# Outer-product attention and a squareplus MLP on one core: the attention of later row blocks is dealt between the MLP's matmuls

## The chip, the core and the metric

The kernel runs on one core of a Trainium2 chip. Its engines are TensorE (PE; its weight loads are shown apart as PEld), VectorE (DVE), ScalarE (ACT), GpSimd (POOL) and SyncE (SP, which here only issues transfers). The metric is the device time of one execution in microseconds (us); the median of several runs counts.

## What is computed

```python
f = 1.0 / (1.0 + np.exp(-f_logit))                     # q, k, v, f_logit: [4, 8, 768, 48]
for t in range(S):
    state = f[:, :, t, :, None] * state + np.einsum('bhd,bhe->bhde', k[:, :, t], v[:, :, t])
    y[:, :, t] = np.einsum('bhd,bhde->bhe', q[:, :, t], state)
x = y.transpose(0, 2, 1, 3).reshape(3072, 384)
h = x @ w_in                                           # w_in [384, 2048], w_out [2048, 384]
out = (0.5 * (h + np.sqrt(h * h + 4.0))) @ w_out
```

The recurrence is worked out in chunks of 128 tokens. Within a chunk the running sum of ln(1 + exp(-f_logit)) over the tokens scales q down and k up, so that a masked product of the two gives the chunk's own part, and a state of 48 by 48 per head carries the rest from chunk to chunk.

## The kernel before

There are two stages, one after the other. **Attention** goes by batch `b` (four, each of 768 tokens, 8 heads, 6 chunks). L87 to L90 load one batch of the four inputs; L108 and L111 take Exp and Ln of the whole batch; then, head by head, L119 forms the running sums `ca` in fp32 on PE, L124 and L126 take their two exponentials, L129 and L130 multiply q and k with them on POOL into `qkg`, and L134 to L142 form the chunk's decay `gam`. After that come 3 x 8 rounds of (chunk pair, head), each with tiles of 48 rows or 48 columns: transposes (L154, L155), their copy by ACT (L156), scores (L158), the mask on DVE (L160), the product with v (L163), the product with the state (L166), the new state (L170 to L177), and the cast of the result into `xT` by ACT (L181). In `xT` each head has 64 rows, 48 of them used, so that the first weight has four K tiles for 384 rows (L96 to L106 lay it out so).

**The MLP** goes by blocks of 512 tokens (L189, six of them). For each of 16 column tiles, four matmuls of 128x512 (L195) are followed by Square and Sqrt on ACT (L200, L201) and one operation on DVE (L202) that makes `g`; then four output tiles of 16 matmuls each (L208), their copy (L212) and the store (L213). Its buffers in PSUM are taken only when those of the attention are given back (L183). The order of the engines' work is the scheduler's, by the dependencies and the buffers of the pools.

Of the kernel before, what the change touches and what calls it, by code (L numbers as in the profile page):

```python
# [12 lines left out]


@with_exitstack
def kernel(
# [41 lines left out]
    w_in16 = konst.tile([128, NP, DFF], FP16)
    w_out16 = konst.tile([128, NN, DM], FP16)

    xT = konst.tile([128, NP, NTOK], FP16)

    actx = ExitStack()
    pp_ca = actx.enter_context(tc.tile_pool(name="pp_ca", bufs=1, space=bass.MemoryType.PSUM))
    pp_nl = actx.enter_context(tc.tile_pool(name="pp_nl", bufs=1, space=bass.MemoryType.PSUM))
    pp_tr = actx.enter_context(tc.tile_pool(name="pp_tr", bufs=2, space=bass.MemoryType.PSUM))
    pp_py = actx.enter_context(tc.tile_pool(name="pp_py", bufs=2, space=bass.MemoryType.PSUM))
# [176 lines left out]
```

## Time and profile before

| | |
|---|---|
| median of 3 runs | 463.24 us (463.15 to 464.77) |
| span of the profiled execution, first to last instruction | 459.8 us |
| attention stage, 0 to 305 us: PE, DVE, ACT busy | 241.4, 131.3, 139.4 us |
| MLP stage, 305 to 459.8 us: PE, DVE, ACT busy | 149.1, 75.7, 100.0 us |
| PE busy over the whole span | 390.5 us (85%), 2304 matmuls |
| moved by transfers | 30.3 MB |

The profiled execution's own device time is not listed apart from its span; the median is 3.4 us longer than that span, and those 3.4 us are taken to lie before the first and behind the last instruction. A busy PE is not a PE at its peak: a matmul is counted from its first operand read to its modelled end, so overlapping short matmuls fill the line while the array does little. The distance from one start to the next says more.

### The profile page before, as it was taken

How to read it: one execution, taken by the hardware profiler on the slowest of the kernel's cores; microseconds unless marked ns; L12 is line 12 of the kernel's file. 1: busy time of each engine (PE TensorE's matmuls, PEld its weight loads, DVE VectorE, ACT ScalarE, POOL GpSimd, SP SyncE). 2: the span in 40 equal slices, each digit the busy share in tenths (PEclk: the TensorE clock that was granted, in tenths of full speed). 3: DMA queues.
4: the chain of work that ended last, by engine and by line, in shares of the span. 5: the costliest groups of instructions: out<-in, count | busy, mean ns of one | idle time of the engine just before them, and what ended most of it. 6: DMA issues, size and time to landing. Idle time of an engine off the chain costs nothing.

```text
span 459.8 us, 6306 instructions
## 1 busy us (share of the span) xinstructions
PE 390.5 (85%) x2304; PEld 217.6 (47%) x2304; DVE 207.0 (45%) x639; ACT 239.4 (52%) x498; POOL 70.7 (15%) x84
## 2 busy tenths in 40 slices
PE   0064034999999999998999999999999999999997
PEld 0033012656565565645656555534545454544543
DVE  4353015543435623466433464426364554546362
ACT  1440022684445944458644464459292947658390
POOL 6042008101224011171022220000000000000000
PEclk9999999999999999997555555569999999999999
DMA  8999995790006950007300000000101000010101
GB/s 247 227 187 175 152 177 103 135 175 2 0 2 125 184 106 0 2 0 142 66 1 1 0 1 1 2 0 0 70 0 53 18 36 34 19 51 2 70 0 70
DMA packets 30896, 30.30 MB, mean 66 GB/s; under 512 B 784, under 2 KB 30480, under 8 KB 30480
## 3 DMA queue, kind: packets, MB, share of 16 engines
q1 hardware_dynamic: 28288, 23.60, 25.9%
q10 hardware_dynamic: 2576, 6.29, 6.7%
q8 instruction: 18, 0.29, 0.3%
q14 instruction: 14, 0.11, 0.1%
HBM read 25.17 MB, written 4.72 MB: 65 GB/s over the span
## 4 chain that ended last, share of the span: by engine, by line
PE 73%; DMA 9%; ACT 5%; SPq 5%; DVE 3%; POOL 2%; issue 2%; DVEq 0%; ACTq 0%
PE ht L195 14%; PE op L208 14%; DMA vb<-in_v_dram 9%; PE py L166 8%; PE ca L119 7%; PE py L163 7%; PE py L158 6%; PE nl L134 5%; PE tr L154 5%; PE tr L155 4%; SPq L88 3%; PE kv L170 3%; ACT hsq L200 2%; ACT r L201 2%; SPq L89 1%
## 5 line engine op out<-in xcount | busy, mean ns | idle before, releaser
L195 PE MATMUL ht<-xT,w_in 128*128 128x512 f16 x384 | 91.9, 386 | 2.2 <-DVE g L202 2.2
L202 DVE SCALAR_TENSOR_TENSOR g<-ht,r 128x512 f16<-128x512 f32 x96 | 62.3, 687 | 46.9 <-ACT r L201 46.9
L160 DVE TENSOR_TENSOR pmt<-py,mask 128x256 f16<-128x256 f32 x96 | 40.3, 423 | 84.1 <-PE py L158 83.3
L200 ACT ACTIVATE hsq<-ht 128x512 f16<-128x512 f32 x96 | 53.9, 629 | 43.3 <-PE ht L195 43.2
L181 ACT CAST xT<-py 48x256 f16<-48x256 f32 x96 | 34.9, 363 | 73.0 <-PE py L166 67.6
L208 PE MATMUL op<-w_out,g 128*128 128x384 f16 x384 | 69.3, 326 | 0.1
L166 PE MATMUL py<-qkT,shat 48*48 48x128 f16 x160 | 47.5, 297 | 21.4 <-DVE shat L177 21.3
L119 PE MATMUL ca<-lsb,wcent 128*128 128x288 f32 x64 | 41.9, 758 | 25.3 <-ACT lsb L111 24.2
L195 PEld LDWEIGHTS <-w_in 128*128 128x128 f16 x384 | 37.5, 98 | 48.8 <-issue 8.1
L155 PE MATMUL tr<-ident,qkg 128*48 128x128 f16 x192 | 50.2, 306 | 11.6 <-POOL qkg L130 11.6
L201 ACT ACTIVATE r<-hsq 128x512 f16<-128x512 f16 x96 | 57.8, 673 | 0.3
L156 ACT COPY qkT<-tr 48x512 f16<-48x512 f16 x96 | 54.1, 577 | 6.5 <-PE kv L170 3.0
L163 PE MATMUL py<-pmt,v16b 128*48 128x128 f16 x192 | 51.8, 300 | 1.1 <-POOL v16b L114 0.6
L208 PEld LDWEIGHTS <-g 128*128 128x128 f16 x384 | 36.9, 98 | 29.2 <-DVE g L202 3.4
L154 PE MATMUL tr<-ident,qkg 128*48 128x128 f16 x192 | 49.2, 297 | 0.2 <-POOL qkg L129 0.2
L129 POOL TENSOR_TENSOR qkg<-qb,ea 128x288 f16<-128x288 f32 x32 | 25.3, 792 | 137.6 <-ACT ea L124 137.6
L177 DVE TENSOR_SCALAR shat<-tmps,gam 48x48 f16<-48x48 f32 x160 | 41.9, 285 | 0.9 <-DVE tmps L174 0.2
L166 PEld LDWEIGHTS <-shat 48*48 48x48 f16 x160 | 17.9, 112 | 44.3 <-DVE shat L177 22.3
L158 PE MATMUL py<-qkT 48*128 48x128 f16 x192 | 37.7, 293 | 0.0
L134 PEld LDWEIGHTS nl<-hvec,lsb 128*48 128x48 f32 x384 | 34.0, 193 | 5.4 <-issue 3.2
L134 PE MATMUL nl<-hvec,lsb 128*48 128x2 f32 x384 | 35.9, 220 | 0.5 <-DVE nlsb L139 0.5
L163 PEld LDWEIGHTS <-v16b 128*48 128x48 f16 x192 | 23.1, 129 | 24.6 <-issue 15.0
(41 smaller groups left out, 317.0 us busy)
## 6 DMA issues: line engine op xcount, KB each, us to landing
out_dram<-o_sb SPq DMA_DIRECT2D x24, 192.0 KB, 1.9
w_out_f<-in_moe_w_out_dram ACTq DMA_DIRECT2D x1, 3072.0 KB, 16.5
w_in_f<-in_moe_w_in_dram ACTq DMA_DIRECT2D x8, 384.0 KB, 13.0
flb<-in_f_logit_dram SPq DMA_DIRECT2D x4, 0.2 KB, 16.4
qb<-in_q_dram SPq DMA_DIRECT2D x4, 0.2 KB, 10.6
kb<-in_k_dram SPq DMA_DIRECT2D x4, 0.2 KB, 14.6
vb<-in_v_dram SPq DMA_DIRECT2D x4, 0.2 KB, 12.2
```

What stands on the lines that cost most here:

```text
L119: nc.tensor.matmul(out=ca.rearrange("p c d -> p (c d)"), lhsT=wcent, rhs=lsb[:, h].rearrange("p c d -> p (c d)"), start=True, stop=True)
L134: nc.tensor.matmul(out=nl[:, c, :], lhsT=lsb[:, h, c, :], rhs=hvec, start=True, stop=True)
L154: nc.tensor.transpose(out=tr[:, 0, cc, :], in_=qkg[:, h, c, 0:D], identity=ident16)
L155: nc.tensor.transpose(out=tr[:, 1, cc, :], in_=qkg[:, h, c, D:2 * D], identity=ident16)
L158: nc.tensor.matmul(out=pt[:, cc, :], lhsT=qkT[:, 1, cc, :], rhs=qkT[:, 0, cc, :], start=True, stop=True)
L163: nc.tensor.matmul(out=y[:, cc, :], lhsT=v16b[:, h, c, :], rhs=pmt[:, cc, :], start=True, stop=(c == 0))
L166: nc.tensor.matmul(out=y[:, cc, :], lhsT=shat[:, h, c, :], rhs=qkT[:, 0, cc, :], start=False, stop=True)
L195: nc.tensor.matmul(out=ht, lhsT=w_in16[:, j, jn * 128:(jn + 1) * 128], rhs=xT[:, j, tok0:tok0 + MB], start=(j == 0), stop=(j == NP - 1))
L200: nc.scalar.activation(out=hsq, in_=ht, func=AF.Square, scale=1.0)
L201: nc.scalar.activation(out=r16, in_=hsq, func=AF.Sqrt, scale=0.25, bias=1.0)
L202: nc.vector.scalar_tensor_tensor(out=g16[:, jn, :], in0=ht, scalar=0.5, in1=r16, op0=ALU.mult, op1=ALU.add)
L208: nc.tensor.matmul(out=op, lhsT=g16[:, jn, tg * 128:(tg + 1) * 128], rhs=w_out16[:, jn, :], start=(jn == 0), stop=(jn == NN - 1))
```

## The change

The kernel is written anew around row blocks of 128 tokens over all 8 heads (24 of them, 12 pairs). Heads are taken in pairs, each with 64 of 128 columns, so that a transpose or a state product covers two heads (`st_T`, `st_SC`, `st_KV`, `st_Y`); the result is transposed back (`st_YT`) to a dense `xT` of three K tiles. The running sums are two fp16 matmuls, of the high and the low part of the logarithm, in place of one fp32 matmul. Exp and Ln come in seven groups of row blocks (`window`), with a table load ahead of each and one behind. The MLP goes by pairs of row blocks (256 tokens): `mlp1` in eight halves of six 128x256 matmuls, the second matmul (`mlp2`) in quarters of four. The driver issues one group's window, and then the `mlp1` of the group before with the attention steps of the new group between its halves; quarters of `mlp2` fill the windows. The four PSUM tiles `hps` serve `mlp1` and the running sums; four more serve everything else. Weights are loaded in quarters behind the first inputs. The order of ACT is the written one; that of the others is the scheduler's.

```diff
+GROUPS = [(0, 2), (2, 4), (4, 6), (6, 10), (10, 16), (16, 22), (22, 24)]
...
+    ctx.enter_context(tc.manual_schedule(engines={mybir.EngineType.Activation}))
...
+    qt = [konst.tile([128, PR, H, 64], FP16, name=f"qt{i}") for i in range(NB)]
+    kt = [konst.tile([128, PR, H, 64], FP16, name=f"kt{i}") for i in range(NB)]
...
+    hps = [pp_h.tile([128, 512], FP32, name=f"hps{i}") for i in range(4)]
...
+    def load_pair(p):
...
+            for r in range(PR):
+                b, c = divmod(p * PR + r, NC)
+                nc.sync.dma_start(out=got[name][:, r],
+                                  in_=src[b][:, c * C:(c + 1) * C, :].rearrange("h t d -> t h d"))
...
+    def load_w_in(i):
...
+        nc.sync.dma_start(out=s3, in_=moe_w_in[:, i * WQ:(i + 1) * WQ].rearrange("(j p) n -> p j n", p=128))
+        nc.scalar.copy(out=w_in16[:, :, i * WQ:(i + 1) * WQ], in_=s3)
...
+        def exp_ln(p):
...
+            nc.scalar.activation(out=f, in_=f, func=AF.Exp, scale=-1.0)
+            nc.scalar.activation(out=ls, in_=f, func=AF.Ln, bias=1.0, scale=1.0)
+            hi, lo = lhi[p % 2], llo[p % 2]
+            nc.vector.tensor_copy(out=hi[:, :, :, 0:D], in_=ls)
+            nc.vector.tensor_tensor(out=lo[:, :, :, 0:D], in0=ls, in1=hi[:, :, :, 0:D], op=ALU.subtract)
...
+            nc.gpsimd.tensor_copy(out=v16, in_=loads[p]["v"])
...
+        def cums(p):
...
+            for r in range(PR):
+                ca = hp2[r][:, 0:H * D]
+                nc.tensor.matmul(out=ca, lhsT=wcent, rhs=hi[:, r, :, 0:D], start=True, stop=False)
+                nc.tensor.matmul(out=ca, lhsT=wcent, rhs=lo[:, r, :, 0:D], start=False, stop=True)
...
+            for r in range(PR):
+                ca = hp2[r][:, 0:H * D]
+                nc.scalar.activation(out=ea[:, r].rearrange("p h d -> p (h d)"), in_=ca, func=AF.Exp, scale=-1.0)
+                nc.scalar.activation(out=eap[:, r].rearrange("p h d -> p (h d)"), in_=ca, func=AF.Exp, scale=1.0)
+            nc.gpsimd.tensor_tensor(out=qt[p % NB][:, :, :, 0:D], in0=ld["q"], in1=ea, op=ALU.mult)
+            nc.gpsimd.tensor_tensor(out=kt[p % NB][:, :, :, 0:D], in0=ld["k"], in1=eap, op=ALU.mult)
...
+                for hp in range(NP):
+                    o = nl[:, hp, :]
+                    nc.tensor.matmul(out=o, lhsT=hi[:, r, 2 * hp:2 * hp + 2, :], rhs=hvec, start=True, stop=False)
+                    nc.tensor.matmul(out=o, lhsT=lo[:, r, 2 * hp:2 * hp + 2, :], rhs=hvec, start=False, stop=True)
+                nc.vector.tensor_copy(out=nls[b % 2][:, c + r], in_=nl)
...
+    def st_T(r):
...
+        tr = pp_a.tile([128, 2 * NP, C], FP16, name="tr", tag="a")
+        for j in range(NP):
+            nc.tensor.transpose(out=tr[:, j, :], in_=qt[p % NB][:, i, 2 * j:2 * j + 2, :], identity=ident16)
+            nc.tensor.transpose(out=tr[:, NP + j, :], in_=kt[p % NB][:, i, 2 * j:2 * j + 2, :], identity=ident16)
+        qkT = bp.tile([128, 2 * NP, C], FP16, name="qkT", tag="qkT")
+        nc.vector.tensor_copy(out=qkT, in_=tr)
...
+    def st_SC(r):
...
+        for s in range(2):
+            sc = pp_a.tile([128, NP, C], FP32, name="sc", tag="a")
+            o = 64 * s
+            for j in range(NP):
+                nc.tensor.matmul(out=sc[:, j, :], lhsT=qkT[o:o + D, NP + j, :], rhs=qkT[o:o + D, j, :],
...
+            nc.vector.tensor_tensor(out=pm[:, s], in0=sc, in1=mask16.unsqueeze(1).broadcast_to([128, NP, C]),
...
+    def st_KV(r):
...
+        u = pp_a.tile([128, NP, 2, D], FP32, name="u", tag="a")
+        if c > 0:
+            nc.tensor.matmul(out=u.rearrange("p a b d -> p (a b d)"), lhsT=ident16,
+                             rhs=state[r].rearrange("p a b d -> p (a b d)"), start=True, stop=False)
+        for j in range(NP):
+            nc.tensor.matmul(out=u[:, j], lhsT=kt[p % NB][:, i, 2 * j:2 * j + 2, :],
+                             rhs=v16s[p][:, i, 2 * j:2 * j + 2, :], start=(c == 0), stop=(c == 0 or j == NP - 1))
+        sn = bp.tile([128, NP, 2, D], FP16, name="sn", tag="sn")
+        nc.vector.tensor_tensor(out=sn, in0=u,
+                                in1=gam[b % 2][:, c].unsqueeze(3).broadcast_to([128, NP, 2, D]), op=ALU.mult)
...
+    def st_Y(r):
...
+        y = pp_a.tile([128, NP, 2, D], FP32, name="y", tag="a")
+        for j in range(NP):
+            if c > 0:
+                nc.tensor.matmul(out=y[:, j], lhsT=qkT[:, j, :], rhs=state[r][:, j], start=True, stop=False)
+            for s in range(2):
+                nc.tensor.matmul(out=y[:, j, s], lhsT=pm[:, s, j, :], rhs=v16s[p][:, i, 2 * j + s, :],
+                                 start=(c == 0), stop=(c == 0 or s == 1))
+        y16 = bp.tile([128, NJ, 128], FP16, name="y16", tag="y16")
+        nc.vector.tensor_copy(out=y16.rearrange("p a b -> p (a b)"), in_=y.rearrange("p a b d -> p (a b d)"))
...
+    def st_YT(r):
...
+        for j in range(NJ):
+            nc.tensor.transpose(out=yt[:, j, :], in_=part[r]["y16"][:, j, :], identity=ident16)
...
+        nc.vector.tensor_copy(out=xTs[p][:, :, i * C:(i + 1) * C], in_=yt)
...
+        for i in range(n):
+            r = r0 + i
+            at.setdefault(4 * i, []).append((None, lambda r=r: st_T(r)))
+            at.setdefault(4 * i + 2, []).append((None, lambda r=r: st_SC(r)))
+            at.setdefault(4 * i + 5, []).append((None, lambda r=r: st_Y(r)))
+            if (r + 1) % NC and r + 1 < r1:
+                at.setdefault(4 * i + 3, []).append((None, lambda r=r: st_KV(r)))
+            if r == r0 and r % NC:
+                at.setdefault(0, []).append((None, lambda r=r: st_KV(r - 1)))
+            at.setdefault(4 * i + 8, []).append((r, lambda r=r: st_YT(r)))
...
+        def half(j2):
...
+            hb = hps[j2 % 4].rearrange("p (a t) -> p a t", a=2)
+            for a in range(2):
+                jn = 2 * j2 + a
+                for j in range(NJ):
+                    nc.tensor.matmul(out=hb[:, a, :], lhsT=w_in16[:, j, jn * 128:(jn + 1) * 128],
+                                     rhs=x[:, j, :], start=(j == 0), stop=(j == NJ - 1))
...
+        def elem(j4):
...
+            for a in range(2):
+                nc.scalar.activation(out=hsq[:, a, :], in_=hps[(2 * j4 + a) % 4], func=AF.Square, scale=1.0)
             nc.scalar.activation(out=r16, in_=hsq, func=AF.Sqrt, scale=0.25, bias=1.0)
...
+            for a in range(2):
+                jn = 4 * j4 + 2 * a
+                nc.vector.scalar_tensor_tensor(out=g16[:, jn:jn + 2, :].rearrange("p a t -> p (a t)"),
+                                               in0=hps[(2 * j4 + a) % 4], scalar=0.5, in1=r16[:, a, :],
+                                               op0=ALU.mult, op1=ALU.add)
...
+            def quarter(n, i=i, box=box):
...
+                for jn in range(4 * n, 4 * n + 4):
+                    nc.tensor.matmul(out=o, lhsT=gts[p][:, jn, i * C:(i + 1) * C], rhs=w_out16[:, jn, :],
+                                     start=(jn == 0), stop=(jn == NN - 1))
...
+                    nc.vector.tensor_copy(out=o_sb, in_=o)
+                    t0 = (p * PR + i) * C
+                    nc.sync.dma_start(out=out[t0:t0 + C, :], in_=o_sb)
...
+    def run_window(g, per=1):
+        nc.scalar.preload_act_table_set("natural_log_exp_and_others")
+        for s in window(g):
+            s()
+            fill_some(per)
+        nc.scalar.preload_act_table_set("sqrt_and_others")
...
+            for n, s in enumerate(mlp1(p)):
+                s()
+                if n % 3 != 2:
+                    k_half += 1
+                    want = natt * k_half // nhalf
+                    if not att:
+                        fill_some(1)
+                    while att and natt - len(att) < want:
+                        att_slot()
+            fill.extend(mlp2(p))
...
+    more_loads(2)
+    run_window(0)
+    run_window(1)
+    for i in range(4):
+        load_w_in(i)
+    more_loads(3)
+    while att:
+        att_slot()
+    run_mlp1(0)
+    for i in range(4):
+        load_w_out(i)
+    more_loads(6)
+    run_mlp1(1)
+    run_window(2, 2)
+    while att:
+        att_slot()
+        fill_some(2)
+    run_window(3, 2)
+    run_mlp1(2)
+    for g in range(3, NG):
+        if g + 1 < NG:
+            run_window(g + 1, 2)
+        run_mlp1(g)
+    while fill:
```

Three places show how it stands now. First PE in the middle of the program. Before, in the attention stage, a round of one head and two chunks:

```order
L163 LDWEIGHTS v16b
L163 MATMUL py<-pmt,v16b 48x128
L166 LDWEIGHTS shat
L166 MATMUL py<-qkT,shat 48x128
L158 LDWEIGHTS qkT
L158 MATMUL py<-qkT 128x128
...
L170 LDWEIGHTS qkg
L170 MATMUL kv<-v16b,qkg 48x48
L154 LDWEIGHTS qkg
L154 MATMUL tr<-ident_58,qkg 48x128
L155 LDWEIGHTS qkg
L155 MATMUL tr<-ident_58,qkg 48x128
```

In the changed kernel, about two thirds through, `hps` being the tiles of the first matmul, `sc` the scores, `u` the new state, `yt` and `tr` transposes:

```order
L299 LDWEIGHTS w_in_104
L299 MATMUL hps_137<-xT,w_in_104 128x256
...
L218 LDWEIGHTS qkT
L218 MATMUL sc<-qkT 128x128
...
L229 LDWEIGHTS ident_87
L229 MATMUL u<-sn,ident_87 128x384
L232 LDWEIGHTS kt_111
L232 MATMUL u<-v_1966,kt_111 128x96
...
L299 MATMUL hps_138<-xT,w_in_104 128x256
...
L299 MATMUL hps_139<-xT,w_in_104 128x256
...
L258 LDWEIGHTS y_2399
L258 MATMUL yt<-ident_87,y_2399 128x128
```

What moved: the first matmul of the MLP, which stood behind all attention, now stands between the steps of later row blocks, six at a time, and the steps are 128 columns wide.

Second DVE at the same place, `g` made for the MLP, the others for attention. Before, in the attention stage:

```order
L141 TENSOR_TENSOR gamin<-tmp_1753,nlsb 48x5
L140 TENSOR_TENSOR tmp_1775<-nlsb 48x6
L139 COPY nlsb<-nl 48x12
L160 TENSOR_TENSOR pmt<-py,mask_69 128x256
L176 TENSOR_TENSOR tmps<-kv,shat 48x48 x2
...
L177 TENSOR_SCALAR shat<-tmps,gam 48x48 x2
```

and in the changed kernel:

```order
L310 SCALAR_TENSOR_TENSOR g_2322<-hps_138,r_2402 128x512
L310 SCALAR_TENSOR_TENSOR g_2322<-hps_139,r_2402 128x512
L220 TENSOR_TENSOR pm<-sc,mask_92 128x512 x2
L235 TENSOR_TENSOR sn<-u,gam_119 128x384
L310 SCALAR_TENSOR_TENSOR g_2322<-hps_136,r_2442 128x512
L310 SCALAR_TENSOR_TENSOR g_2322<-hps_137,r_2442 128x512
L261 COPY xT<-yt 128x3x128
L208 COPY qkT<-tr 128x1024
L251 CAST y_2490<-y 128x384
```

What moved: DVE makes `g` and the attention's tiles in one queue, two of `g` at a time, and each pair stands behind Sqrt on ACT; the copy `qkT`, which was ACT's, is now DVE's.

Third PE early in the program, in the second pair's first matmul (`o` is an output tile, `g_471` the first pair's `g`):

```order
L299 MATMUL hps_137<-xT,w_in_104 128x256
L328 LDWEIGHTS g_471
L328 MATMUL o<-w_out_105,g_471 128x384
...
L299 LDWEIGHTS w_in_104
L299 MATMUL hps_138<-xT,w_in_104 128x256
```

What moved: the first quarter of the second matmul, which needs the first quarter of `w_out`, stands ahead of halves of the first matmul that don't; the other three quarters follow within the next 130 matmuls. Before, the whole of `w_out` had been loaded and cast long ahead of its first use.

## Rows read from the trace of the kernel before

**Rows 1.** Busy time by stretch: length, PE, PEld, DVE, ACT, POOL, clock, DMA, GB/s

```profile
0.00:305.00 305.00, 241.37 (x1543) 143.82 (x1544) 131.29 (x519) 139.36 (x304) 70.72 (x84) 0.85 0.45 83
305.00:459.80 154.80, 149.14 (x762) 73.80 (x762) 75.72 (x120) 100.04 (x194) 0.00 (x0) 0.99 0.09 31
```

**Rows 2.** The page's chain that ended last, share of the span by engine

```profile
PE 73%; DMA 9%; ACT 5%; SPq 5%; DVE 3%; POOL 2%; issue 2%; DVEq 0%; ACTq 0%
```

**Rows 3.** Busy time by stretch again, columns as in rows 1, for TensorE's pace

```profile
80.00:200.00 120.00, 117.05 (x777) 72.10 (x778) 55.09 (x263) 67.23 (x149) 26.64 (x33) 1.00 0.39 70
...
208.00:210.00 2.00, 1.40 (x14) 0.87 (x13) 1.31 (x6) 0.92 (x3) 1.15 (x2) 1.00 0.01 2
212.00:300.00 88.00, 87.29 (x549) 50.99 (x547) 40.63 (x191) 47.30 (x105) 12.48 (x16) 0.50 0.13 23
...
309.00:460.00 151.00, 145.79 (x752) 72.64 (x751) 75.33 (x120) 96.11 (x189) 0.00 (x0) 1.00 0.09 32
```

**Rows 4.** Timeline of PE in the attention stage: start us, duration us, line, tiles

```profile
202.89 0.31 PE L154 MATMUL tr<-ident,qkg 128*48 128x128 f16 x1
202.99 0.31 PE L155 MATMUL tr<-ident,qkg 128*48 128x128 f16 x1
...
205.28 0.22 PE L154 MATMUL tr<-ident,qkg 128*48 128x128 f16 x1
205.34 0.22 PE L155 MATMUL tr<-ident,qkg 128*48 128x128 f16 x1
...
216.68 0.30 PE L166 MATMUL py<-qkT,shat 48*48 48x128 f16 x1
216.91 0.30 PE L163 MATMUL py<-pmt,v16b 128*48 128x128 f16 x1
```

**Rows 5.** Chain of work in order of time, one MLP block: start, length

```profile
336.42 1.89 PE ht L195 x8
...
348.48 7.49 PE op L208 x45
```

**Rows 6.** Timeline of one MLP block's beginning: start us, duration us, engine, line

```profile
306.17 0.15 PEld L195 LDWEIGHTS <-w_in 128*128 128x128 f16 x1 [0.28 <-issue]
306.59 0.15 PEld L195 LDWEIGHTS <-w_in 128*128 128x128 f16 x1 [0.28 <-issue]
...
311.89 1.16 ACT L201 ACTIVATE r<-hsq 128x512 f16<-128x512 f16 x2
312.56 1.29 DVE L202 SCALAR_TENSOR_TENSOR g<-ht,r 128x512 f16<-128x512 f32 x2 [0.72 <-ACT r L201]
...
313.88 1.18 ACT L201 ACTIVATE r<-hsq 128x512 f16<-128x512 f16 x2
```

**Rows 7.** Groups by line: shapes, count, busy us, mean ns, idle before

```profile
L202 DVE SCALAR_TENSOR_TENSOR g<-ht,r 128x512 f16<-128x512 f32 x96 | 62.3, 687 | 46.9 <-ACT r L201 46.9
...
L160 DVE TENSOR_TENSOR pmt<-py,mask 128x256 f16<-128x256 f32 x96 | 40.3, 423 | 84.1 <-PE py L158 83.3
...
L129 POOL TENSOR_TENSOR qkg<-qb,ea 128x288 f16<-128x288 f32 x32 | 25.3, 792 | 137.6 <-ACT ea L124 137.6
...
L212 DVE COPY o_sb<-op 128x384 f32<-128x384 f32 x24 | 13.4, 558 | 31.9 <-PE op L208 31.9
L124 ACT ACTIVATE ea<-ca 128x288 f32<-128x288 f32 x32 | 13.1, 410 | 36.4 <-PE ca L119 36.2
...
L98 DVE CAST w_out<-w_out_f 128x6144 f16<-128x6144 f32 x1 | 3.4, 3361 | 9.8 <-DMA w_out_f<-in_moe_w_out_dram 9.8
```

**Rows 8.** Busy time by stretch, columns as in rows 1, while inputs load

```profile
30.00:40.00 10.00, 7.03 (x62) 5.59 (x62) 3.57 (x10) 1.64 (x4) 5.91 (x6) 1.00 1.12 188
40.00:60.00 20.00, 0.68 (x5) 0.40 (x5) 0.25 (x2) 0.00 (x0) 0.04 (x1) 1.00 1.05 159
```

**Rows 9.** Timeline of ACT between Exp and Ln: start us, duration us

```profile
20.49 1.28 ACT L111 ACT_TABLE_LOAD   x1
21.79 2.12 ACT L111 ACTIVATE lsb<-lsb 128x2304 f32<-128x2304 f32 x1
```

More of the change, by code (lines that the diff above doesn't have):

```diff
@@ L12 @@
 ALU = mybir.AluOpType
+PSUM = bass.MemoryType.PSUM
+GROUPS = [(0, 2), (2, 4), (4, 6), (6, 10), (10, 16), (16, 22), (22, 24)]
 @with_exitstack
@@ L58 @@
[L58 to L67, printed above, removed]
@@ new lines @@
+    llo = [konst.tile([128, PR, H, 64], FP16, name=f"llo{i}") for i in range(2)]
+    gam = [konst.tile([128, NC, NP, 2], FP32, name=f"gam{i}") for i in range(2)]
+    nls = [konst.tile([128, NC, NP, 2], FP32, name=f"nls{i}") for i in range(2)]
+    for t in lhi + llo:
+        nc.vector.memset(t[:, :, :, D:64], 0.0)
+    for t in gam:
+        nc.vector.memset(t, 0.0)
+    for t in qt + kt:
+        nc.gpsimd.memset(t[:, :, :, D:64], 0.0)
+    hps = [pp_h.tile([128, 512], FP32, name=f"hps{i}") for i in range(4)]
@@ new lines @@
+    state = {}
+    xTs = {}
+    part = {}
+    def st_T(r):
+        p, i = divmod(r, PR)
+        tr = pp_a.tile([128, 2 * NP, C], FP16, name="tr", tag="a")
[4 more added lines that the diff above has]
+        nc.vector.tensor_copy(out=qkT, in_=tr)
+        part[r] = {"qkT": qkT}
@@ new lines, in mlp2 @@
+    def mlp2(p):
+        steps = []
+        for i in range(PR):
+            box = {}
+            def quarter(n, i=i, box=box):
+                if n == 0:
+                    box["o"] = pp_a.tile([128, DM], FP32, name="o", tag="a")
+                o = box["o"]
+                for jn in range(4 * n, 4 * n + 4):
+                    nc.tensor.matmul(out=o, lhsT=gts[p][:, jn, i * C:(i + 1) * C], rhs=w_out16[:, jn, :],
+                                     start=(jn == 0), stop=(jn == NN - 1))
+                if n == 3:
+                    o_sb = mp.tile([128, DM], FP32, name="o_sb", tag="o_sb")
+                    nc.vector.tensor_copy(out=o_sb, in_=o)
+                    t0 = (p * PR + i) * C
+                    nc.sync.dma_start(out=out[t0:t0 + C, :], in_=o_sb)
+            steps += [lambda n=n, q=quarter: q(n) for n in range(4)]
+        return steps
@@ new lines, with more_loads, att_slot, fill_some @@
+    NG = len(GROUPS)
+    pairs_of = [list(range(a // PR, b // PR)) for a, b in GROUPS]
+    nload = 0
+    def more_loads(upto):
+        nonlocal nload
+        while nload < min(upto, NRB // PR):
+            load_pair(nload)
+            nload += 1
+    att = []
+    done_x = set()
+    fill = []
+    def att_slot():
+        if att:
+            for r, s in att.pop(0):
+                s()
+                if r is not None:
+                    done_x.add(r)
+    def fill_some(n):
+        for _ in range(n):
+            if fill:
+                fill.pop(0)()
@@ new lines @@
+    more_loads(2)
[13 more added lines that the diff above has]
+    while att:
+        att_slot()
+        fill_some(2)
[6 more added lines that the diff above has]
+    while fill:
+        fill_some(1)
```

276 lines of the change are left out of this document (130 added, 146 removed).

## The prediction

> **What bounds the kernel now.** I read the busy time by stretch first. The program has two halves that don't overlap: attention to about 305 us, the MLP for the 155 us after it [rows 1]. The chain of waits says that PE carries 73% of it [rows 2]. But the reader should not take that for a PE at its limit. In the attention stage PE shows 117 of 120 us busy with 777 matmuls between 80 and 200 us [rows 3], that is 0.15 us each, for tiles of 128 columns or fewer. The timeline shows why: back-to-back transposes start 0.10 us apart at 202.9 us and 0.06 apart at 205.3, and where a product with the state (48 rows) and one with v (128 rows) alternate, the starts lie 0.23 us apart [rows 4]. So small tiles and a slow clock fill this stage. The record of the clock says 1.00 from the start, but the pace at 202.9 us is that of 0.50 further on; only from about 205 to 212 us is it the faster one. I read it so: the attention stage runs at the lower level (1.2 GHz) except for those 7 us, which end after a stretch with PE 1.40 of 2.00 us busy; after that the record says 0.50 to 300 us and the pace is 549 matmuls in 88 us, about the same as before [rows 3]. In the MLP stage, dense from 309 us, it stays at 1.00 (2.4 GHz) to the end [rows 3].
>
> **Prices.** *PE*: eight 128x512 matmuls take 1.89 us and forty-five 128x384 take 7.49 us [rows 5], so 0.166 us for 384 columns and 0.11 for 256 at the upper level; at the lower one 512 columns go 0.42 us apart (the weight loads of 306.17 and 306.59 us [rows 6]), so 0.21 for 256 and 0.32 for 384. An attention step is 0.06 or 0.107 us [rows 4]; the alternation at 0.23 is the upper bound, nothing below 0.055 is seen. A row block has 36 of them (8 in `st_T`, 8 in `st_SC`, 5 in `st_KV`, 12 in `st_Y`, 3 in `st_YT`): 2.2 us at the upper level, 3.9 at the lower, 8.3 at the bound. I take the spacing of transposes, since all but the 8 scores use all rows of the array. *ACT*: Square and Sqrt of two 512-column tiles repeat every 1.99 us [rows 6], which is the price of one `elem`; there are 48, 96 us. Exp of 288 columns is 0.41 us [rows 7], 0.5 for 384, and of 768 about 0.8, a third of 2.12 with its fixed part [rows 9]. *DVE*: two `g` operations take 1.29 us [rows 6]; a 256-column product from PSUM 0.42, a 384-column copy 0.56 [rows 7], so 0.69 for 512 and 1.22 for the 1024 columns of `qkT`. With two masks and three 384-column tiles a row block costs DVE 4.3 us; back to back I take 4.2. The cast of 6144 columns at 0.55 ns each [rows 7] puts a lower bound of 0.6 us on `qkT`; I take the upper, as its source is in PSUM like L212's. *POOL*: 288 columns are 0.79 us [rows 7], 768 then 2.1, two per pair. *Transfers*: 188 and 159 GB/s with nothing but such 192-byte runs in flight [rows 8]; I take 180, so 8.7 us for a pair's 1.57 MB.
>
> What is removed: two fp32 passes of the running sums, 96 rounds of one head, ACT's copies (L156, L181), and a quarter of the first matmul (three K tiles for four: 576 matmuls of 0.11 us are 63 us, for 384 of 0.22, 83 us). What is added: 24 identity products for the state, 72 transposes back, the split into high and low parts (two DVE passes of 768 columns, 1.4 us a pair). Table loads go from 10 to 14. Each is 1.28 us with ACT's next instruction right behind it, 20.49 to 21.79 us [rows 9], so 18 us in all, some of it while PE does `mlp2`. The Trainium skill, ScalarE: Activation LUTs, What ACT_TABLE_LOAD costs, counts about 2.7 us for a switch, a drain included, and advises to batch by table set; by that the fourteen would be 37 us. Here the trace has no gap around the load, so the row's price stands.
>
> Sums by engine: PE 198 us at the upper level (63 + 64 for the second matmul + 52 for 24 row blocks + 19 for the running sums) and 375 at the lower; DVE 200 (62 + 101 + 13 for the output copies + 24 for windows and casts); ACT 167 (96 + 24 + 19 + 18 + 10). None is near 460, and all three are needed at once, so I sum stretch by stretch in the order of the program.
>
> - **Opening, 92 us.** The third piece of PE's order decides it. Ahead of the last quarter of `w_out` the queue moves pairs 0 to 2, `w_in`, `w_out` and a bit, 11.2 MB: 62 us. The first matmul of pairs 0 and 1 lies under this (their attention is through at 41 us, bound by Exp, POOL and DVE). PE has then some 27 queued 384-column matmuls, 0.32 each at the lower level: 8. The second window's running sums, exponentials and POOL: 6. Two row blocks with nothing beside them: 8 us of latency (2.7 us of T, scores and masks, 2.6 of their DVE work, Y and its transposes 2.7) and 4.2 for the second: 12. The first sums of the next window: 4.
> - **Group (6, 10) with `mlp1` of pair 2, 26 us**: DVE 8 x 0.645 + 4 x 4.2 = 22, PE 26 at the lower level, 14 at the upper. PE is not dense here, so I take the lower.
> - **Group (10, 16), 12 + 42 us.** Of the window 12 us show: table, four Exp/Ln (4.5), `mlp2` matmuls that stand ahead of the sums on PE (2.6), two exponentials pairs (2), POOL (4.2), less overlaps. Then six row blocks with 16 halves: DVE 10.3 + 25.2 = 36, PE 24 or 44. I take 42.
> - **Group (16, 22), 11 + 49 us**: DVE 15.5 + 25.2 = 41, PE 30 or 57; 49 lies between, for an engine that waits in order for two others.
> - **Last group, 7 + 62 us.** One pair's window, and then `mlp1` of four pairs, two row blocks and 13 or 14 output tiles: PE 4 x 5.3 + 4.4 + 36 = 62 at the upper level, as dense as the MLP stage is now; ACT's 32 lie under it.
> - **End, 3 us**: the last copy and store.
>
> That is 304 us of span. Its counterpart is 459.8, and what lies around it, 3.4 us by the median of the runs, comes on top: **307 us**.
>
> **Rivals.**
> *All well overlapped, 259 us.* PE gets to the upper level in the mixed stretches, DVE copies `qkT` and `xT` faster than L212's pace, windows vanish behind `mlp2`: 85 + 20 + 9 + 31 + 8 + 36 + 5 + 58 + 3 = 255. For it: ACT and DVE each total 200 us or less. Against it: DVE and PE wait for each other in order, four `hps` tiles are two `elem` deep, and PE fell back to the lower level at 212 us after short idle times [rows 3]. The Trainium skill, VectorE: DVE Perf Modes, The perf-mode tier table, allows a copy from PSUM up to twice the base rate; by it `qkT` would cost some 0.65 us and a row block 3.5, with 17 us less on DVE in all. No row here has a 16-bit copy from PSUM on DVE.
> *Dealt in name only, 337 us.* The change doesn't do what it says: attention and MLP take turns, because each step waits for DVE while DVE's head waits for Sqrt (`g` at the head of its queue in the second place shown). Then a row block costs its chain of some 6 us and each `mlp1` its 8.2: 92 + 32 + 12 + 52 + 11 + 61 + 7 + 64 + 3 = 334. For it: DVE's 46.9 us of waiting for L201 [rows 7] are that wait in the MLP before, where nothing stands behind it. Against it: the order gives most steps two or more halves of distance.
> *Lower level to the end, 386 us.* The MLP bursts of six never bring the clock up: 95 + 28 + 13 + 46 + 12 + 59 + 9 + 118 + 3 = 383. Against it: the last group is as dense as the stage that holds 1.00 now.
> *Slower than before, about 500 us.* One mechanism: every one of the 1,065 matmuls outside the MLP starts 0.23 us after the last, as where tile heights alternate [rows 4], at the lower clock: 245 + 247 for the MLP + 16 until the first tile = 508. It decides from 0.19 us each on. Against it: runs of equal height are at 0.10 or 0.06.
>
> **How the numbers follow.** Chances: my forecast 0.45 (its own range 288 to 326), all overlapped 0.26, dealt in name only 0.20, lower level 0.06, slower 0.02, other 0.01. The range of 264 to 352 us takes in the first, the third and half or more of the second, with the unknown prices of `qkT` and of the attention's matmuls, and leaves out 2 in 10. Changes under 0.5% can't be told from none here. Every case but one is far below 461 us: faster 0.97, same 0.01, slower 0.02.
>
> **What would show it.** Right: the last `w_out` cast near 62 us and the second window's Exp just behind; DVE and PE both over 80% busy from 130 to 230 us; a clock that changes level in the mixed stretches and stays at 1.00 over the last 60; about 200 us of DVE. `qkT` rows tell the DVE price, the spacing in `st_Y` the PE price. Wrong: DVE waiting for L307 and PE for DVE in turn for tens of us (in name only); a window that leaves all engines idle for 15 us; or a later group's inputs that are not there when its Exp comes, since loads of pairs 6 and 7 stand behind stores in SP's queue.

## The result, and the profile after

The kernel after takes 271.11 us (median of 4 runs, 269.83 to 271.85), the kernel before beside it 463.59: a ratio of 0.585 (95% interval 0.583 to 0.587). The profiled execution took 270.39 us, its span is 268.6. Ratios here and below rest on undisturbed executions alone. The forecast of 307 us was 36 too long: the time lies inside the range, but below the 288 to 326 us that the likeliest case had for itself.

The page of the kernel after (busy time by engine; PE, DVE and the clock in 40 slices of 6.7 us; the chain by engine):

```profile
span 268.6 us, 5160 instructions
PE 213.1 (79%) x2024; PEld 148.9 (55%) x2024; DVE 182.7 (68%) x332; ACT 169.3 (63%) x252; POOL 57.5 (21%) x52
...
PE   0366939897688775986886869999886999999995
...
DVE  1456726863583899579999666999983697645521
...
PEclk9999995999555997999999989999998899999999
...
PE 32%; DVE 22%; ACT 16%; DMA 10%; issue 8%; SPq 6%; POOL 4%; POOLq 1%; ACTq 0%; DVEq 0%
```

PE carries 32% of the chain now, where it carried 73% [rows 2]; DVE and ACT share it. DVE reads 9 from 121 to 148 and from 168 to 195 us (slices 18 to 21 and 25 to 28, counted from 0), PE without a break from 208 us on (slice 31). The clock is down to 0.5 from 40 to 47 and from 67 to 87 us. The row reads 9 for the first 32 us too, but the spacing of the transposes speaks against it:

```profile
17.07 0.31 PE L205 MATMUL tr<-ident,qt 128*128 128x128 f16 x1
17.17 0.31 PE L206 MATMUL tr<-ident,kt 128*128 128x128 f16 x1
...
178.50 0.22 PE L205 MATMUL tr<-ident,qt 128*128 128x128 f16 x1
178.56 0.22 PE L206 MATMUL tr<-ident,kt 128*128 128x128 f16 x1
```

0.10 and 0.06 us apart are the two paces of [rows 4], so PE ran at the lower level (1.2 GHz) at 17 us, as the prediction reads it for the kernel before, whose row reads 9 there too.

The same execution by the stretches of the prediction's sum (columns as in rows 1; a window is taken from DVE's last copy or `g` of the group before to about its first `qkT`):

```profile
0.00:85.50 85.50, 57.40 (x484) 38.04 (x485) 45.73 (x92) 49.43 (x71) 23.20 (x31) 0.85 1.04 197
85.50:105.40 19.90, 13.48 (x167) 9.96 (x166) 18.96 (x34) 14.81 (x20) 3.29 (x3) 0.93 0.60 118
105.40:118.00 12.60, 11.14 (x103) 6.87 (x102) 9.03 (x15) 6.02 (x14) 7.13 (x5) 0.91 1.40 198
118.00:147.50 29.50, 22.87 (x303) 17.86 (x300) 28.29 (x53) 22.66 (x35) 7.75 (x7) 1.00 1.04 165
147.50:165.20 17.70, 14.81 (x128) 8.92 (x127) 11.41 (x18) 8.98 (x21) 11.73 (x6) 0.90 0.10 35
165.20:197.60 32.40, 30.06 (x360) 23.84 (x359) 31.87 (x59) 29.08 (x39) 0.82 (x1) 1.00 0.01 2
197.60:206.00 8.40, 5.06 (x47) 2.90 (x44) 4.30 (x9) 4.67 (x9) 3.56 (x2) 1.00 0.13 47
206.00:265.60 59.60, 58.25 (x447) 40.56 (x447) 32.77 (x56) 33.68 (x49) 0.01 (x1) 0.97 0.11 41
265.60:268.60 3.00, 0.00 (x0) 0.00 (x0) 0.30 (x1) 0.00 (x0) 0.00 (x0) 0.90 0.18 66
```

| stretch | predicted | measured |
|---|---|---|
| opening | 92 | 85.5 |
| (6, 10) with `mlp1` of one pair | 26 | 19.9 |
| window, (10, 16) with two pairs | 12 + 42 | 12.6 + 29.5 |
| window, (16, 22) with three pairs | 11 + 49 | 17.7 + 32.4 |
| window, the rest | 7 + 62 | 8.4 + 59.6 |
| end | 3 | 3.0 |

The three mixed stretches gave 35.2 us less than predicted, the opening 6.5 less, the windows 8.7 more. In the mixed stretches DVE is busy for 79.1 of 81.8 us. What it does there, on its timeline (start, length):

```profile
179.96 0.34 DVE L261 COPY xT<-yt 128x384 f16<-128x384 f16 x1
180.22 0.68 DVE L208 COPY qkT<-tr 128x1024 f16<-128x1024 f16 x1
180.82 0.54 DVE L251 CAST y<-y 128x384 f16<-128x384 f32 x1
181.29 1.27 DVE L310 SCALAR_TENSOR_TENSOR g<-hps,r 128x512 f16<-128x512 f32 x2
182.48 1.27 DVE L220 TENSOR_TENSOR pm<-sc,mask 128x512 f16<-128x512 f32 x2
183.68 0.54 DVE L235 TENSOR_TENSOR sn<-u,gam 128x384 f16<-128x384 f32 x1
184.14 1.27 DVE L310 SCALAR_TENSOR_TENSOR g<-hps,r 128x512 f16<-128x512 f32 x2
185.34 0.34 DVE L261 COPY xT<-yt 128x384 f16<-128x384 f16 x1
```

From one `xT` to the next it is 5.38 us: one row block and four `g`, and each instruction starts as the one before ends or a little sooner (`qkT` 0.26 us after `xT`, which is 0.34 long). By this DVE sets the pace; the doubled copy below tests it.

### The profile page after: what moved, and what is told of

It is laid out like the page before. It is cut to its first block, busy times and chain, and to the rows that moved or that the text cites. A ratio compares the mean times of both kernels' runs of the same rounds, so it can differ in the third digit from the quotient of the medians.

```text
span 268.6 us, 5160 instructions
## 1 busy us (share of the span) xinstructions
PE 213.1 (79%) x2024; PEld 148.9 (55%) x2024; DVE 182.7 (68%) x332; ACT 169.3 (63%) x252; POOL 57.5 (21%) x52
## 4 chain that ended last, share of the span: by engine, by line
PE 32%; DVE 22%; ACT 16%; DMA 10%; issue 8%; SPq 6%; POOL 4%; POOLq 1%; ACTq 0%; DVEq 0%
PE o L328 16%; PE hps L299 10%; SPq L104 6%; DVE g L310 6%; ACT hsq L306 4%; DVE pm L220 3%; ACT r L307 3%; DMA ld_v<-in_v_dram 3%; DMA ld_f<-in_f_logit_dram 3%; DMA w_st<-in_moe_w_in_dram 3%; DVE qkT L208 2%; DVE llo L138 2%; POOL kt L158 2%; DVE y L251 2%; ACT L371 2%
## 5 line engine op out<-in xcount | busy, mean ns | idle before, releaser
L299 PE MATMUL hps<-xT,w_in 128*128 128x256 f16 x576 | 80.5, 285 | 10.6 <-DVE g L310 9.7
L310 DVE SCALAR_TENSOR_TENSOR g<-hps,r 128x512 f16<-128x512 f32 x96 | 61.8, 682 | 20.5 <-ACT r L307 20.5
L328 PE MATMUL o<-w_out,g 128*128 128x384 f16 x384 | 73.0, 335 | 0.2 <-DVE w_out L120 0.2
L299 PEld LDWEIGHTS <-w_in 128*128 128x128 f16 x576 | 57.0, 102 | 23.5 <-issue 13.2
L306 ACT ACTIVATE hsq<-hps 128x512 f16<-128x512 f32 x96 | 54.5, 590 | 23.4 <-PE hps L299 22.3
L307 ACT ACTIVATE r<-hsq 128x1024 f16<-128x1024 f16 x48 | 50.7, 1057 | 1.5
L328 PEld LDWEIGHTS <-g 128*128 128x128 f16 x384 | 37.6, 100 | 23.4 <-issue 3.3
L157 POOL TENSOR_TENSOR qt<-ld_q,ea 128x768 f16<-128x768 f32 x12 | 22.7, 1892 | 82.4 <-ACT ea L155 72.6
L220 DVE TENSOR_TENSOR pm<-sc,mask 128x512 f16<-128x512 f32 x48 | 30.9, 682 | 4.2 <-PE sc L218 4.2
L158 POOL TENSOR_TENSOR kt<-ld_k,eap 128x768 f16<-128x768 f32 x12 | 22.4, 1866 | 0.0
L205 PE MATMUL tr<-ident,qt 128*128 128x128 f16 x96 | 16.7, 245 | 4.6 <-POOL qt L157 3.8
```

The costliest lines, as they stand in the source:

```text
L157: nc.gpsimd.tensor_tensor(out=qt[p % NB][:, :, :, 0:D], in0=ld["q"], in1=ea, op=ALU.mult)
L158: nc.gpsimd.tensor_tensor(out=kt[p % NB][:, :, :, 0:D], in0=ld["k"], in1=eap, op=ALU.mult)
L205: nc.tensor.transpose(out=tr[:, j, :], in_=qt[p % NB][:, i, 2 * j:2 * j + 2, :], identity=ident16)
L220: nc.vector.tensor_tensor(out=pm[:, s], in0=sc, in1=mask16.unsqueeze(1).broadcast_to([128, NP, C]), op=ALU.mult)
L299: nc.tensor.matmul(out=hb[:, a, :], lhsT=w_in16[:, j, jn * 128:(jn + 1) * 128], rhs=x[:, j, :], start=(j == 0), stop=(j == NJ - 1))
L306: nc.scalar.activation(out=hsq[:, a, :], in_=hps[(2 * j4 + a) % 4], func=AF.Square, scale=1.0)
```

## The experiments

Each is the kernel after with the edit shown, timed against the kernel before; "below" and "above after" compare the two ratios. The table splits each profiled span at the loads of the Sqrt table behind the windows of (6, 10), (10, 16), (16, 22) and (22, 24) (us):

| kernel | to 1st | to 2nd | to 3rd | to 4th | to the end | median |
|---|---|---|---|---|---|---|
| after | 87.7 | 34.4 | 42.9 | 39.8 | 63.8 | 271.1 |
| attention in one piece | 86.8 | 38.8 | 52.4 | 50.6 | 51.8 | 282.2 |
| `qkT` copied twice | 87.1 | 38.7 | 47.1 | 43.0 | 65.2 | 283.5 |
| four K tiles | 92.3 | 35.6 | 46.7 | 42.4 | 71.6 | 288.0 |
| `qt`, `kt` on DVE | 85.0 | 34.5 | 40.9 | 39.9 | 61.2 | 263.5 |
| a quarter of the weights | 82.2 | 35.8 | 43.0 | 41.4 | 65.3 | 268.5 |
| single heads | 87.1 | 36.0 | 44.4 | 39.8 | 64.7 | 273.7 |
| early dealing | 79.1 | 36.4 | 43.4 | 39.8 | 64.4 | 265.0 |

**Attention in one piece.**

```diff
         att.extend(attention(g))
+        if g >= 2:
+            while att:
+                att_slot()
-    xp = ... name="xp", bufs=5
+    xp = ... name="xp", bufs=6
```

> The kernel after, with each group's attention issued in one piece behind its window instead of being dealt between the halves of the MLP of the group before (one more buffer for xT). Theory A, the overlap is the gain: 18 row blocks at about 4 us (the spacing of two row blocks alone in the opening of the kernel after, plus latency) are no longer beside 6 pairs of MLP, so the stretches from 85 to 206 us (121 us now) become about 150, and the time about 300 us, 290 to 320. Theory B, the gain comes from the denser tiles and the cheaper steps alone and the dealing adds little: 268 to 276 us.

282.17 us, ratio 0.610 (0.608 to 0.613), 11 us above after: between the theories, and nearer to B. The DVE timeline of its third attention, and then the stretch of this attention and that of the MLP behind it:

```profile
183.41 0.35 DVE L261 COPY xT<-yt 128x384 f16<-128x384 f16 x1
183.67 0.68 DVE L208 COPY qkT<-tr 128x1024 f16<-128x1024 f16 x1
184.27 0.55 DVE L251 CAST y<-y 128x384 f16<-128x384 f32 x1
184.84 1.29 DVE L220 TENSOR_TENSOR pm<-sc,mask 128x512 f16<-128x512 f32 x2
186.04 0.55 DVE L235 TENSOR_TENSOR sn<-u,gam 128x384 f16<-128x384 f32 x1
186.51 0.35 DVE L261 COPY xT<-yt 128x384 f16<-128x384 f16 x1
```

```profile
178.00:195.00 17.00, 11.59 (x174) 8.28 (x172) 16.85 (x34) 6.08 (x9) 0.00 (x0) 0.97 0.01 2
195.00:219.90 24.90, 24.90 (x185) 18.44 (x184) 14.58 (x24) 20.82 (x31) 0.00 (x0) 0.95 0.07 24
```

A row block alone takes 3.10 us here, from one `xT` (183.41) to the next (186.51), and DVE has no gap: DVE sets the pace of the attention by itself too. And the MLP alone is not a chain that waits: PE is 24.9 of 24.9 us busy from 195 us, because `mlp2` of earlier pairs stands between the halves. The table shows the trade: without dealing the second, third and fourth parts grow by 4.4, 9.5 and 10.8 us, and the rest gains 12.0, since part of the second matmuls is done by then.

**`qkT` copied twice.**

```diff
+        qkT2 = bp.tile([128, 2 * NP, C], FP16, name="qkT2", tag="qkT2")
+        nc.vector.tensor_copy(out=qkT2, in_=tr)
         nc.vector.tensor_copy(out=qkT, in_=tr)
```

> The kernel after, with the copy of the eight transposes (qkT, 0.68 us) done twice, the first time into a tile that nobody reads: DVE pays about 1.3 us per row block, a little over what the prediction assumed (1.22). Theory A, DVE sets the pace of the mixed stretches (it is 79 of 82 us busy there): 16 row blocks times 0.6 us, 10 us more, and up to 4 for the six row blocks of the opening: 280 to 285 us. Theory B, the forecast missed by the clock and by waits, not by DVE's prices: 270 to 274 us.

283.53 us, ratio 0.613 (0.609 to 0.618): A. Parts two to four of the table grow by 4.3, 4.2 and 3.2 us, 11.7 for 16 row blocks at 0.6 to 0.7 us. In the second and third part the clock is lower as well; in the fourth, near 1.00 in both kernels, it is 3.2 us for 6 copies. So DVE's time is paid in full there, and the forecast's price for `qkT` (1.22 us for 0.68, 16 times) was worth some 9 to 10 of its 36 us.

**Four K tiles.**

```diff
-    NJ = DM // 128
+    KP = 96
+    NJ = DM // KP
```

(and 96 in place of 128 rows in `w_in16`, `y16`, `yt` and `xT`).

> The kernel after, with four K tiles of 96 rows in the first matmul instead of three of 128 (768 matmuls of 256 columns for 576, 96 transposes back for 72). Theory A, PE sets the pace only in the last 60 us and DVE before: 4 pairs times 16 matmuls at 0.11 us is 7, 3 more in the stretch before, where PE is 30 of 32 us busy, 1 for the wider xT copies: about 282 us, 278 to 286. Theory B, PE sets the pace from 85 us on: 10 pairs times 1.76 us and 3 for the transposes, 20 us or more: 290 to 295. Theory C, PE is slack everywhere: 271.

288.0 us, ratio 0.621 (0.617 to 0.625), 17 above after: between A and B. The profiled execution is 2.4 us above the median, so its parts add up to more. The last part grows by 7.8, as A has it, the third and fourth by 3.8 and 2.6 for 3.5 and 5.3 us that PE has more to do (32 and 48 matmuls at 0.11 us); but also the opening by 4.6, which A left out: two pairs with 16 matmuls more are 3.5 us at the upper level's price and 6.7 at the lower one's, 0.21 us. In the third part the clock is lower, too, 0.88 for 0.96 in the kernel after; in the fourth, at 1.00 in both, half of what PE has more to do is paid. PE stands close behind DVE.

**`qt` and `kt` on DVE.**

```diff
-            nc.gpsimd.tensor_tensor(out=qt[p % NB]...
-            nc.gpsimd.tensor_tensor(out=kt[p % NB]...
+            nc.vector.tensor_tensor(out=qt[p % NB]...
+            nc.vector.tensor_tensor(out=kt[p % NB]...
```

> The kernel after, with the two products of 768 columns per pair (qt and kt) on DVE instead of POOL. In the window of group (16, 22) DVE's two split passes take 1.73 and 2.44 us while POOL multiplies, 0.56 and about 0.9 while it does not. Theory A, POOL slows DVE and is itself slow (1.85 us each against about 0.8 expected on DVE), and the windows are a chain of both: the three late windows of 12.6, 17.7 and 8.4 us lose 2 to 5 us each, 258 to 267 us. Theory B, DVE is the engine in need and 12 times 1.6 us more on it cost more than the windows give back: 274 to 288 us.

263.50 us, ratio 0.569 (0.566 to 0.572), 2.7% below after: A in the total, but not as A had it. The three parts with the late windows lose nothing, 2.0 and nothing; 2.7 come from the opening and 2.6 from the end. From table load to table load the windows of two and three pairs are 4.3, 0.8 and 3.0 us shorter ((6, 10), (10, 16), (16, 22)) and those of one pair 0.3 to 1.1 longer; the stretches between pay part of it back. What the edit does inside a window shows in the rows. In the kernel after, DVE and then POOL in the window of (16, 22):

```profile
153.44 0.76 DVE L180 TENSOR_TENSOR gi<-nls 128x8 f32<-128x8 f32 x1
...
154.64 1.73 DVE L137 CAST lhi<-ls 128x768 f16<-128x768 f32 x1
156.41 2.44 DVE L138 TENSOR_TENSOR llo<-ls,lhi 128x768 f16<-128x768 f32 x1
```

```profile
154.14 1.82 POOL L158 TENSOR_TENSOR kt<-ld_k,eap 128x768 f16<-128x768 f32 x1
155.94 2.09 POOL L157 TENSOR_TENSOR qt<-ld_q,ea 128x768 f16<-128x768 f32 x1
158.00 2.51 POOL L158 TENSOR_TENSOR kt<-ld_k,eap 128x768 f16<-128x768 f32 x1
```

and DVE there in this kernel:

```profile
153.90 0.55 DVE L137 CAST lhi<-ls 128x768 f16<-128x768 f32 x1
154.37 0.16 DVE L180 TENSOR_TENSOR gi<-nls 128x8 f32<-128x8 f32 x1
154.49 0.96 DVE L138 TENSOR_TENSOR llo<-ls,lhi 128x768 f16<-128x768 f32 x1
155.36 0.95 DVE L157 TENSOR_TENSOR qt<-ld_q,ea 128x768 f16<-128x768 f32 x1
```

`lhi` starts at 154.64 beside POOL's `kt` and ends at 156.37, 0.41 us after `kt` has; `llo` ends 0.82 us after POOL's next product. Each looks as if it had begun only when POOL was done. With POOL idle they take 0.55 and 0.96, a `gi` 0.16 for 0.76, and the product itself 0.95 for 1.8 to 2.5.

**A quarter of the weights.**

```diff
-        nc.sync.dma_start(out=s3, in_=moe_w_in[...
+        if i == 0:
+            nc.sync.dma_start(out=s3, in_=moe_w_in[...
```

(the same for `moe_w_out`; three quarters of each weight are left out, and the one that is loaded is cast four times).

> The kernel after, with one quarter of each weight transferred and cast four times: 4.7 of 30.2 MB are left out, and the values in the other three quarters are wrong. Theory A, the opening is bounded by transfers (16 engines' share about 1.0 to 85 us, about 200 GB/s): the 4.7 MB are worth up to 23 us of it, and the work of PE, 57 us in the opening at a clock of 0.85, becomes the next bound: 250 to 258 us. Theory B, the opening is a chain of Exp, POOL, DVE and a slow PE with the transfers beside it: 268 to 271 us.

268.5 us, ratio 0.580 (0.576 to 0.583): B. The end of the opening in this kernel, and in the kernel after:

```profile
58.00:85.00 27.00, 18.15 (x174) 12.26 (x174) 14.59 (x30) 13.62 (x25) 13.48 (x9) 0.66 0.51 101
```

```profile
58.00:85.00 27.00, 21.25 (x180) 13.24 (x179) 14.89 (x28) 14.45 (x24) 10.11 (x7) 0.66 1.20 184
```

The DMA share of this stretch falls from 1.20 to 0.51, and PE does nearly the same there (174 and 180 matmuls, both at a clock of 0.66). The opening is 5.5 us shorter for 4.7 MB less, 23 us at 200 GB/s, and by the medians 2.6 us of that are left at the end. Full DMA engines were no sign of a bound here.

**Single heads.**

```diff
-            nc.tensor.transpose(out=tr[:, j, :], in_=qt[p % NB][:, i, 2 * j:2 * j + 2, :], ...
+            nc.tensor.transpose(out=tr[o:o + 64, j, :], in_=qt[p % NB][:, i, h, :], ...
```

(the same for `kt` and for `u`; the first row block of a sequence adds a state of zeros).

> The kernel after, with the transposes of qt and kt and the products of kt with v taken one head at a time again: 16 and 8 small steps instead of 8 and 4, 12 more per row block, 288 in all, at 0.06 to 0.107 us 17 to 31 us more of PE; DVE's work is the same. Theory A, PE stands so close behind DVE that most of what is added there is paid, as with four K tiles: 280 to 290 us. Theory B, DVE sets the pace of the row blocks and the small steps fit beneath it: 270 to 275 us.

273.65 us, ratio 0.592 (0.590 to 0.594), 2.5 above after: B. But the test is weaker than meant, as the page's PE row shows:

```profile
PE 221.8 (82%) x2300; PEld 150.0 (55%) x2300; DVE 181.6 (67%) x333; ACT 169.7 (62%) x252; POOL 57.8 (21%) x52
```

276 more matmuls are 8.7 us more of PE (213.1 above), 0.03 us each and not 0.06 to 0.107. Its transposes show why:

```profile
181.32 0.23 PE L209 MATMUL tr<-ident,kt 128*64 128x128 f16 x2
181.38 0.23 PE L208 MATMUL tr<-ident,qt 128*64 128x128 f16 x2
```

Two half-wide ones, for the two halves of `tr`, are over in 0.23 us together, where one whole takes 0.22, and the next two follow after 0.06 us, as the next whole one does in the kernel after. So taking the heads one by one gave PE hardly more steps in time, and this run can't price them.

**fp32 sums.**

```diff
-                nc.tensor.matmul(out=ca, lhsT=wcent, rhs=hi[:, r, :, 0:D], start=True, stop=False)
-                nc.tensor.matmul(out=ca, lhsT=wcent, rhs=lo[:, r, :, 0:D], start=False, stop=True)
+                nc.tensor.matmul(out=ca, lhsT=wcent32, rhs=l32[:, r, :, 0:D], start=True, stop=True)
```

(the same for `nl`; `hi` and `lo` go).

> The kernel after, with the running sums taken in fp32 again: one fp32 matmul of 384 columns per row block for two fp16 ones, one fp32 matmul of 2 columns for each fp16 pair, and neither of DVE's two split passes (1.9 us a pair by their means). Theory A, the windows are a chain in which the split stands on the path and costs more than fp32 does on PE (about 1.0 us for 384 columns at the lower clock, from 0.76 for 288 in the kernel before, against 0.64 for the fp16 pair): five windows lose 1 to 3 us each, 258 to 267 us. Theory B, the fp32 passes on PE, which stand in a queue with the second matmuls, cost more than DVE gives back: 24 row blocks times 0.4 us and more, 274 to 282 us.

Ratio 0.579 (0.576 to 0.582), which stands for 268.0 us: about 1% below after and just beyond A's end. It rests on two executions of four (267.95 and 268.10 us); the other two took 272.86 and 277.05. A gain of the high/low form is not to be seen in this kernel, and neither is a loss.

**Last two groups joined, on top of `qt`, `kt` on DVE.**

```diff
-GROUPS = [..., (10, 16), (16, 22), (22, 24)]
+GROUPS = [..., (10, 16), (16, 24)]
```

> The kernel with qt and kt on DVE, with the last two groups joined (16 to 24): one window and two table loads fewer. Theory A, a window costs what PE lacks in it (the last one of the kernel after is 8.4 us long with PE busy for 5.1) and joining saves that: about 260 us, 258 to 262. Theory B, eight row blocks now stand beside three pairs of MLP where DVE sets the pace, two more at 3 us each, while the last four pairs of MLP run with nothing beside them: 264 to 268 us.

261.64 us, ratio 0.565 (0.563 to 0.567): A, at its upper end, 0.7% below the kernel that it is built on.

**`y` on ACT, on top of `qt`, `kt` on DVE.** 

```diff
-        nc.vector.tensor_copy(out=y16...
+        nc.scalar.copy(out=y16...
```

> The kernel with qt and kt on DVE, with the copy of y (128x384 from PSUM, 0.55 us on DVE) on ACT. Theory A, DVE sets the pace and ACT has room: 10 to 16 row blocks times 0.5 us, 255 to 259 us. Theory B, ACT is nearly as full beside the MLP (29 of 32 us in the kernel after) and takes its orders strictly in turn, so that Square and Sqrt wait behind copies whose matmuls are not done: 264 to 275 us.

280.42 us, ratio 0.605 (0.602 to 0.608): worse than both. Most of it falls in the opening, where B had not looked: the first load behind the window of (6, 10) comes at 96.8 us for 85.0, and the first `xT` at 40.3 for 22.2. ACT issues in the order of the program, and `y` of pair 0 stands behind the table loads, the Exp of pair 1 and the casts of `w_in`.

**Early dealing.**

```diff
-    run_mlp1(1)
     run_window(2, 2)
-    while att:
-        att_slot()
-        fill_some(2)
+    run_mlp1(1)
     run_window(3, 2)
```

> The kernel after, with the window and the two row blocks of group (4, 6) dealt between the halves of pair 1's MLP in the opening, instead of after it with nothing beside them. Theory A, those two row blocks (about 9 us at 69 to 78 us, at a clock of 0.5 to 0.66) go under the MLP: 262 to 267 us. Theory B, ACT takes its orders in turn, the window's Exp and its two table loads stand ahead of pair 1's Square, and PE has nothing in their place: 269 to 276 us.

265.03 us, ratio 0.573 (0.571 to 0.575), 2.0% below after: A. The opening is 8.6 us shorter, and 3.1 are given back behind it. With the test of the weights this suggests that the opening is more a chain of steps that wait for each other than a matter of transfers. The clock has a part in it, too. The rest of the opening from 58 us on:

```profile
58.00:79.10 21.10, 18.60 (x200) 12.66 (x201) 16.43 (x31) 16.25 (x27) 5.22 (x5) 1.00 1.18 190
```

The clock is 1.00 here and 0.66 from 58 to 85 us in the kernel after. How much of the 8.6 us is the clock and how much the overlap, no run took apart.

**Three joined: fp32 sums, `qt` and `kt` on DVE, six groups.**

> Three changes to the kernel after at once: fp32 running sums without DVE's split, qt and kt on DVE, the last two groups joined. Theory A, they add up (2 to 3, 8 and 2 us): 257 to 261 us. Theory B, the first two relieve the same chain in the windows and the fp32 passes make PE, busy for 236 us in the kernel with fp32 sums, the next bound: 262 to 268 us.

274.84 us, ratio 0.593 (0.591 to 0.595): beyond B, and slower than after. It differs from the kernel with six groups by its fp32 sums alone. PE's row of this kernel, and then of that:

```profile
PE 233.5 (86%) x2024; PEld 170.0 (62%) x2024; DVE 178.4 (65%) x331; ACT 167.7 (62%) x248; POOL 13.5 (5%) x28
```

```profile
PE 210.6 (81%) x2024; PEld 148.6 (57%) x2024; DVE 192.1 (74%) x355; ACT 167.2 (64%) x248; POOL 14.5 (6%) x28
```

PE has 23 us more to do. So it had in the kernel with fp32 sums (236.2 us, in its longest execution), without a loss in the shorter two. The window of (16, 24), from table load to table load, is 28.4 us long for 21.5, that of (10, 16) 24.5 for 20.5. My reading is that the split costs much only where POOL keeps DVE out; with POOL idle it is 1.5 us a pair, and only PE's price is left. No run took these two apart further, so this is argued, not shown.

**The version from the experiments: `qt` and `kt` on DVE, six groups, early dealing.**

> Three changes that gained by themselves put together: qt and kt on DVE, the last two groups joined, and the window and row blocks of group (4, 6) dealt into pair 1's MLP. Theory A, the early dealing works in the opening and the other two behind it, so they add up: 6 us below the 261.6 of the first two, 254 to 257 us. Theory B, DVE has the products of pair 2 to do as well as the casts of w_out and g of pair 1 in the opening, and the gain is given back there, as in the kernel with three changes joined: 260 to 268 us.

257.26 us, ratio 0.557 (0.554 to 0.560), 4.8% below after: A, within 0.3 us of it. Of its page:

```profile
span 252.9 us, 5123 instructions
...
PE 203.0 (80%) x2024; PEld 144.7 (57%) x2024; DVE 190.6 (75%) x355; ACT 166.7 (66%) x248; POOL 14.4 (6%) x28
...
PEclk9999995999999997999998899999999999999999
...
PE 40%; DVE 25%; ACT 11%; SPq 9%; DMA 7%; issue 6%; DVEq 0%; ACTq 0%
```

It beats both kernels. Behind the first 38 us, for which the row can't be trusted (as in the kernel after), the clock is at 0.5 in one slice only (38 to 44 us), and PE leads the chain with 40%.

## Why the prediction was right, and where it was off

*What bounds.* That mixing attention with the MLP would bring the clock up is borne out by the clock in the mixed stretches (0.93, 1.00, 1.00); the forecast believed it by halves, and its 26 us for the first of them were PE at the lower level. That attention ran at the lower level before rests on the spacing in [rows 4] alone, and that PE's small steps at a low clock filled that stage was not tested by itself.

*Prices.* The step that failed first is DVE's row block, 4.2 us taken. `qkT` is 0.68 us (1.22 taken), `xT` 0.35 (0.56), the rest as priced, and back to back they take 3.10. 16 row blocks times 1.1 are 18 of the 35 us missing in the mixed stretches; the doubled copy shows that such time is paid, for the 9 to 10 of them that are `qkT`'s. By the rule from the Trainium skill, VectorE: DVE Perf Modes, The perf-mode tier table (up to twice the base rate for a copy from PSUM), `qkT` came to 0.65: the trace agrees. The forecast went by a 32-bit row for a 16-bit copy. The table loads are the row's 1.28 us with the next instruction right behind.

*The stretch sum.* The second failure: on top of DVE's sums of 22, 36 and 41 us the forecast put 18 for waits in order and a slow PE. DVE idled 2.7 us of 81.8 there. With 3.1 us for 4.2 the forecast's own DVE sums come to 17.6, 28.9 and 34.1 us, and 19.9, 29.5 and 32.4 were measured. The windows, 30 us predicted, took 38.7; that POOL holds DVE up in them was not foreseen, but with POOL idle the three late windows are 3.5 us shorter in all from load to load, so what made up the rest stays open. The opening was mis-explained more than mis-sized: of the transfers that were to make 62 of its 92 us, leaving out 4.7 of the 11.2 MB is worth 5.5. The 3.4 us around the span are 1.8 (270.39 less 268.6). The last 62 us, PE-bound, measured 59.6, and four K tiles lengthened it by 7.8 for the 7.0 that 0.11 us a matmul gives.

*The rivals.* The time fits "all well overlapped" (255 of span), whose mixed stretches (20, 31, 36) came within 4 us each; its short windows did not come. The range held because it took in part of this rival, and by luck: with its windows at 30 us the kernel would have come near 262, below the range. The forecast's own case did not come. "In name only" had named the right wait (DVE for L307: 20.5 us here, 46.9 in [rows 7]) and a wrong price: even with no dealing the time is 282 and not 337, as a row block alone takes 3.1 us and not 6, and `mlp2` fills the MLP's waits. Neither lower clock nor slower came.

*What to look for.* The last `w_out` cast began at 56.3 us (62 said). DVE over 80% from 130 to 230 us holds to 195 only, outside the window, and PE reads 6 in three slices of that time; 182.7 us of DVE for 200. Late inputs did not hold up Exp: it waited for a transfer once, for the first tile. PE's small steps were as cheap as priced or cheaper. The transposes start 0.06 us apart (178.50 and 178.56 above), and eight scores, 0.22 us each, start 0.03 us apart on average:

```profile
180.96 0.41 PE L218 MATMUL sc<-qkT 48*128 48x128 f16 x8
```

Eight products with v are over in 0.36 us, the four products with the state and eight with v of a row block in 0.53, and the alternation at 0.23 [rows 4] did not return.

*Where the 192 us came from.* Dealing is worth 11, dense K 17, head pairs in the transposes and in the products of k with v 2.5, the fp16 sums nothing that these runs can show. The other 160, if these add, lie in the attention's new form as a whole, which no run undid: 305 us for 24 row blocks before [rows 1], 12.7 each with windows, against 3.1 and a share of a window. PE tells where they lie: it was busy for 241.4 us of the attention stage, and now attention adds some 60 us to the 153.5 that the page has for the MLP's two lines (L299 and L328; 213.1 in all). Whether fewer and wider steps or the higher clock carries most of that is open.
